# Attention with a mixture of experts on one core: 64 last rows in plain float32, w2 under a name per block, gathered rows turned in two runs

## The chip, the core and the metric

The kernel runs on one core of one Trainium2 chip. The metric is the device time of one execution in microseconds (us), lower is better. An engine is named as in the profile: PE is TensorE's matmuls and PEld its weight loads, DVE is VectorE, ACT is ScalarE, POOL is GpSimd, SP is SyncE, whose queue issues most transfers.

## What is computed

Causal attention with decay over 64 pairs of batch and head (576 positions, head size 64) gives 4608 rows of 512 numbers. Each row goes to one of eight experts, the one with the largest gate value.

```
logits = x @ w_gate                      # 4608 x 512 by 512 x 8
expert_idx = np.argmax(logits, axis=1)
for e in range(E):
    xe = x[expert_idx == e]
    h = np.maximum(xe @ w1[e], 0.0)      # 512 -> 1024
    ye = h @ w2[e]                       # 1024 -> 512
    out[mask] = gate_w[mask, None] * ye
```

## The kernel before

**Stages.** Attention fills the first 310 us; the change leaves it alone. Then eight places of experts follow, numbered e = 0 to 7. Places 2 to 7 hold experts sorted by how many rows they have. Each place has room for a fixed number of rows, `CAPS`: 640 for e = 0 to 3, then 608, 576, 576 and 512.

**Arithmetic.** To keep float32 accuracy with the faster type float32r, a number is split in a rounded part and a rest. A product is then three products: rounded by rounded, rounded by rest, rest by rounded.

**Up and down.** For e = 1 to 7, `seven` computes the hidden values: four rounds i of seven block products (Strassen's scheme) with 28 steps in all. After each of them other work may be inserted, by a table `ups` with the step's number. Then `down` multiplies hidden values with w2, one tile m of 128 rows after the other. A tile is four quarter tiles of six matmuls each (two of the eight row blocks of w2, times three products), 128 columns by 512. A second table, `dns`, says what is inserted after which quarter tile. The tables decide the order in which each engine gets its instructions; each engine works in that order.

**Rows of the next place.** While place e is in its stages, the rows of place e + 1 are gathered: `fetch(e + 1, m)` is an indirect transfer on POOL's queue that brings 128 rows (line 1172). Before, tiles 3 and 4 are fetched after step 6 of the up stage, tile 2 after step 13, tile 0 after step 20, and tile 1 after the first quarter tile of the down stage. `turn_t` transposes a tile on TensorE (four matmuls with the identity, line 1536) into one of two PSUM banks (`ps_t`), from which ACT and DVE build Strassen's sums (lines 1547 to 1561). POOL also adds up blocks of the next place's w1: `sums_s` (lines 1445 to 1448), four additions each, after steps 20 and 27 and after quarter tiles 7 and 14. `split_s` and `split_v` split blocks of w1 and w2: the cast on ACT (lines 1460, 1499), the rest on DVE (lines 1466, 1505).

**w2 in place.** `load_v` brings a block of w2 in float32 (512 KB, SP's queue, line 1485) into a region. `split_v` writes the rounded part to another region and the rest over the float32 values. Two neighbouring blocks share a name in each region; what waits for what is found by names.

**A buffer of the up stage.** In each round, a copy p5 of a product is made on ACT (line 1622), added to on POOL (line 1629) and read by DVE at last (line 1607, `hl<-u`). It has one buffer for all rounds.

Of the kernel before, what the change touches and what calls it, by code (L numbers as in the profile page):

```python
# [18 lines left out]
P = 128  # L19
# [23 lines left out]
NF = 2  # L43
SORTED = E - NF
CAPS = [CAP] * (E - 4) + [608, 576, 576, 512]
XN = ("T2", "T1", "T4", "T3", "B22")
# [65 lines left out]
def two_named(c, nc):  # L112
# [16 lines left out]
    for i, (nm, n) in enumerate(sizes):  # L129
# [3 lines left out]
        elif nm == "xT":  # L133
            name(("xT", i - 2), f"xT{i - 2}", n, at)
        elif nm == "aT":
            name(("aT", i - 5), f"aT{i - 5}", n, at)
            for k, (o, values) in enumerate(((0, False), (HW2, True))):
                name(("w2", i - 5, k), f"w2_{i - 5}_{k}", HW2, at + 4 * o, values)
            name(("hl", i - 5), f"hl{i - 5}", FT * (CA, CB)[i - 5], at, False)
            for k in range(2 * (i - 5)):  # L140
                name(("w1r", k), f"w1r{k}", 8 * P, at + 4 * (FT * CB + 8 * P * k))
        else:
            for k, (a, z) in enumerate(((0, 512), (512, 640))):
                name(("gT", k), f"gT{k}", z - a, at + 4 * a)
# [953 lines left out]
class Moe:  # L1098
# [127 lines left out]
    def sort_table(self):  # L1226
# [5 lines left out]
        for nm, x in (("gi", gi), ("si", si), ("g", g)):  # L1232
# [16 lines left out]
            mine.append(y)  # L1249
        self.idx["sorted"] = tuple(mine)  # L1250

# [84 lines left out]
    def down(self, e, m, part=(0, FT), pool=None):  # L1336
# [19 lines left out]
        self.scatter(y[0:n], si[0:n, s : s + 1])  # L1356


    def down_last(self, e, m):
# [118 lines left out]
    def w2_part(self, names, i, k):  # L1478

        return names["w2", i // 2, k][:, i % 2 * 2 * D : i % 2 * 2 * D + 2 * D]  # L1480

# [45 lines left out]

    def turn_t(self, e, m):

# [3 lines left out]
        xg = self.xg.pop((e, m))  # L1533
        pt = psum(c.ps_t)
        for kt in range(KT):
# [53 lines left out]
    def seven(self, e, i, run, tasks):  # L1589
# [6 lines left out]
        a, b, g, d = (t[:, 0:n] for t in (a, b, g, d))  # L1596
        p1, p5, u2, u3 = (self.up_.tile([P, HN], F32, name=f"u{k}")[:, 0:n] for k in range(4))
        hh, hl = self.h[e]

# [3 lines left out]
        def relu(src, *at):  # L1603
            A.activation(place(hh, *at), src, AF.Relu)

        def rest(src, *at):
            V.scalar_tensor_tensor(place(hl, *at), src, 0.0, place(hh, *at).bitcast(F32),
                                   ALU.max, ALU.subtract)

        def after(s):  # L1610
            if s == 0:
                if e == 1:
                    A.copy(p1, a)
                self.ends.pop(0)()
                if e > 1:
                    A.copy(p1, a)
                self.ends.pop(0)()
# [13 lines left out]
        def end():  # L1631
            relu(d, 1, 0)
            relu(p5, 1, 1)
            V.tensor_tensor(g, g, u2, ALU.add)
            rest(d, 1, 0)
# [8 lines left out]
        self.ends = [end, lambda: relu(g, 0, 1), lambda: (rest(p5, 1, 1), rest(g, 0, 1))]  # L1644

    def run(self, run, rest):
        c, tc = self.c, self.tc
        T = lambda f, *args: lambda: f(*args)
        fetch = lambda e, m: T(lambda: m * P < CAPS[e] and self.fetch(e, m))
        turn_t = lambda e, m: T(lambda: m * P < CAPS[e] and self.turn_t(e, m))  # L1650
        self.s, self.parts, self.slots = {}, {}, 0

        def downs(e, ms, tasks):
            k = 0
            for m in ms:
                for q in range(4):
                    run(lambda: self.down(e, m, (2 * q, 2 * q + 2)))
                    for f in tasks.get(k, []):
# [30 lines left out]
        with tc.tile_pool(name="moe_h", bufs=1) as hp, tc.tile_pool(name="moe_u", bufs=1) as up_, \  # L1689
                tc.tile_pool(name="moe_r", bufs=2) as self.wr:  # L1690
            self.up_ = up_
            hl = hp.tile([P, FT * CAP], F32R, name="hl")
            G = self.nc.gpsimd
            for e in range(1, E):
# [6 lines left out]
                def at(d, *items):  # L1701
# [6 lines left out]
                at(ups, (0, S(self.load_v, 0)), (0, S(self.load_v, 1)),  # L1708
                   (4, S(self.round_s, 2, 1)), (6, S(self.rest_s, 2, 1, G)),
                   (late, S(self.load_v, 2)), (late, S(self.load_v, 3)),  # L1710
                   (8, S(self.split_s, 3, 0)), (9, S(self.split_v, 0)),
                   (11, S(self.round_s, 3, 1)), (13, S(self.rest_s, 3, 1, G)),
                   (15, S(self.split_v, 1)), (v2, S(self.split_v, 2, last)),
                   *[(v3, S(self.split_v, 3))] * (e < E - 1))
                if e == 1:
                    at(ups, (0, S(self.sums_s, 3)), (2, S(self.split_s, 2, 0)))
                if e + 1 < E:
# [203 lines left out]
```

## Time and profile before

| | |
|---|---|
| median of three runs | 731.15 us (729.93 to 731.82) |
| profiled execution, its own time | 730.08 us |
| its span, first to last instruction | 728.1 us |
| PE busy | 718.9 us, 99% |
| DVE, ACT, POOL busy | 553.3, 480.2, 434.1 us |
| mean granted clock of TensorE | 0.999 of 2.4 GHz |

The span is what the trace covers; 2.0 us of the execution lie around it. PE's busy time counts a matmul from its start to its end, and neighbours overlap; what a matmul costs in a stream is the distance of starts.

### The profile page before, as it was taken

To read this page: it belongs to the slowest core of one execution; us is meant where nothing else is said; L and a number is where in the kernel's file an instruction comes from. 1 tells how busy PE (TensorE), PEld (TensorE's weight loads), DVE (VectorE), ACT (ScalarE), POOL (GpSimd) and SP (SyncE) were. 2 spreads that over 40 slices of the span, in tenths; PEclk is the share of its full clock that TensorE was granted. 3 is DMA by queue.
4 is the path that set the end of the run, shared out by engine and by line. 5 is a ranking of instruction groups with operands and counts; after the bars stand their busy time and mean duration, and the time that the engine had idled before them with its cause. 6 is when DMAs were issued, how large, how long until landed. Compare 5 with 4: busy or idle time off the path is not lost. (4 is left out here: it accounts for less than half of the span.)

```text
span 728.1 us, 16528 instructions
## 1 busy us (share of the span) xinstructions
PE 718.9 (99%) x5524; PEld 593.9 (82%) x5524; DVE 553.3 (76%) x1572; ACT 480.2 (66%) x1263; POOL 434.1 (60%) x593
## 2 busy tenths in 40 slices
PE   9999999999999999999999999999999999999996
PEld 6767777777777777889898898898898898898885
DVE  8877989898989899765989478488498498497460
ACT  7899998989898999433666366365365366365431
POOL 6644565656565576835777656566577476576421
PEclk9999999999999999999999999999999999999999
DMA  7988898888888886443383343443433433523301
GB/s 217 251 202 218 217 238 221 230 230 234 219 242 215 225 186 231 146 124 127 102 242 92 139 145 100 135 142 116 144 115 117 167 96 107 174 81 116 134 15 40
DMA packets 82694, 118.16 MB, mean 162 GB/s; under 512 B 9647, under 2 KB 40367, under 8 KB 82608
## 3 DMA queue, kind: packets, MB, share of 16 engines
q1 hardware_dynamic: 75680, 97.18, 48.1%
q0 software_dynamic: 6160, 19.67, 8.1%
q8 instruction: 45, 0.74, 0.4%
q14 instruction: 41, 0.34, 0.2%
q10 hardware_dynamic: 768, 0.25, 0.1%
HBM read 97.88 MB, written 19.63 MB: 161 GB/s over the span
## 5 line engine op out<-in xcount | busy, mean ns | idle before, releaser
L410 ACT ACTIVATE sc<-sc,nmx 128x128 f32<-128x128 f32 (+3 forms) x256 | 143.0, 567 | 2.1 <-DMA wraw<-in_w 1.0
L1583 PE MATMUL ps<-X_0w,w1s 128*128 128x320 f32 (+3 forms) x504 | 105.4, 300 | 0.7 <-ACT u L1622 0.7
L1348 PE MATMUL ps<-w_0w,hhw 128*128 128x512 f32 (+2 forms) x264 | 105.3, 399 | 0.0
L1348 PE MATMUL ps<-w_1w,hhw 128*128 128x512 f32 (+2 forms) x264 | 103.2, 391 | 0.3 <-DVE w_1w L1505 0.3
L1348 PE MATMUL ps<-w_0w,hl 128*128 128x512 f32 (+2 forms) x264 | 103.1, 391 | 0.0
L407 DVE CUSTOM_DVE_ANT_0 sc<-ps,dec 128x384 f32<-128x384 f32 (+2 forms) x192 | 90.2, 506 | 10.6 <-PE ps L423 2.8
L553 PE MATMUL ps<-aT,va_t 128*64 128x256 f32 (+3 forms) x896 | 92.1, 353 | 0.0
L553 PEld LDWEIGHTS ps<-aT,va_t 128*64 128x64 f32 x896 | 57.3, 137 | 31.9 <-issue 6.4
L1583 PEld LDWEIGHTS ps<-X_0w,w1s 128*128 128x128 f32 x504 | 81.7, 188 | 1.5 <-ACT u L1622 1.5
L423 PE MATMUL ps<-raw 64*128 64x256 f32 (+3 forms) x512 | 80.7, 444 | 0.4 <-ACT aT L489 0.4
L1583 PE MATMUL ps<-X_1w,w1s 128*128 128x320 f32 (+3 forms) x252 | 75.3, 299 | 0.0
L1380 POOL DMA_INDIRECT out<-y,so_si x29 | 30.4, 1049 | 72.4 <-ACT y L1355 51.2
L489 ACT COPY aT<-ps 128x512 f32<-128x512 f32 (+4 forms) x154 | 63.0, 453 | 12.5 <-PE ps L493 11.1
L423 PEld LDWEIGHTS ps<-raw 64*128 64x128 f32 x512 | 44.9, 186 | 25.8 <-issue 8.4
L1460 ACT CAST w1s<-w1r 128x1024 fp32r<-128x1024 f32 (+1 forms) x56 | 52.3, 948 | 11.1 <-POOL w1r L1446 10.8
L1466 DVE TENSOR_TENSOR w1s<-w1r,w1s 128x1024 fp32r<-128x1024 f32 (+1 forms) x42 | 52.2, 1257 | 9.2 <-ACT w1s L1460 9.2
L1355 ACT ACTIVATE y<-ps,so_gy 128x512 f32<-128x512 f32 (+2 forms) x28 | 19.3, 690 | 58.9 <-PE ps L1348 42.9
L1348 PEld LDWEIGHTS ps<-w_0w,hl 128*128 128x128 f32 (+2 forms) x264 | 48.5, 184 | 11.8
L1348 PEld LDWEIGHTS ps<-w_1w,hhw 128*128 128x128 f32 (+2 forms) x264 | 48.6, 184 | 10.9 <-DVE w_1w L1505 0.8
L487 DVE COPY aT<-ps 128x384 f32<-128x384 f32 (+4 forms) x118 | 54.2, 493 | 3.6 <-PE ps L493 1.7
L1348 PEld LDWEIGHTS ps<-w_0w,hhw 128*128 128x128 f32 (+2 forms) x264 | 48.5, 184 | 10.2
L1583 PE MATMUL ps<-xa,w1s 128*128 128x320 f32 (+3 forms) x336 | 55.2, 299 | 0.0
(309 smaller groups left out, 1772.9 us busy)
## 6 DMA issues: line engine op xcount, KB each, us to landing
dec<-cd SPq DMA_DIRECT2D x30, 512.0 KB, 5.8
w1r<-in_w SPq DMA_DIRECT2D x112, 128.0 KB, 3.3
w<-in_w SPq DMA_DIRECT2D x28, 512.0 KB, 4.6
raw<-in_qkT SPq DMA_DIRECT2D x63, 160.0 KB, 6.1
raw<-in_qkT SPq DMA_DIRECT2D x64, 144.0 KB, 4.9
decj<-cd SPq DMA_DIRECT2D x30, 288.0 KB, 5.0
va_t<-in_va SPq DMA_DIRECT2D x32, 256.0 KB, 5.7
x_dram<-row SPq DMA_DIRECT2D x32, 256.0 KB, 4.8
```

Source lines behind the costliest of these rows:

```text
L407: V.tensor_tensor_reduce(dst, src, m, -0.125, init, ALU.add, ALU.min, out)
L410: nc.scalar.activation(x, x, AF.Exp, bias=nmx, scale=-1.0, accum_out=acc)
L423: note(nc.tensor.matmul(banks[j][:, o : o + w], r[:, P * t : P * t + P], r[:, QW : QW + w], start=True, stop=n > 1))
L487: V.tensor_copy(dst, src)
L489: nc.scalar.copy(dst, src)
L553: c.last_av = note(nc.tensor.matmul(pv[j * HD : (j + 1) * HD, q0 - qa : qb - qa], l, r, start=(blk == 0), stop=(blk == nb - 1),))
L1348: c.note(nc.tensor.matmul(py, rows(hi_, ft), w[wi], start=(ft + k == 0), stop=(ft == FT - 1 and k == 2),))
L1355: nc.scalar.activation(y[0:n], py, AF.Copy, scale=g[0:n, s : s + 1])
L1380: self.nc.gpsimd.indirect_dma_start(out=self.out, out_offset=bass.IndirectOffsetOnAxis(ap=rows, axis=0), in_=y, in_offset=None, bounds_che ...
L1460: self.nc.scalar.copy(t[:, 0], raw)
L1466: (eng or self.nc.vector).tensor_tensor(lo, raw, hi.bitcast(F32), ALU.subtract)
L1583: self.nc.tensor.matmul(bank, w[:, wi, mat, kt], x[xi][:, kt, :], start=start and k == 0, stop=k == 5, skip_group_check=True,)
```

## The change

**Plain float32 for 64 rows.** Places 5 and 6 have 576 rows, so their fifth tile has 64. `down_few` now multiplies these with w2 in plain float32: no splitting, 16 matmuls of 64 columns by 256 in place of 24 of 64 by 512. The two halves of the 512 outputs go to PSUM partitions 0 to 63 and 64 to 127. The hidden values of these rows are kept unsplit (`keep`, 16 small activations on ACT for each of these places). The unsplit w2 is loaded again for blocks 0 to 2, into the region of the rests, as soon as tile 3 has read them; block 3 is added up from its parts (`whole_v`, DVE). For this, tiles 2 and 3 alternate quarter by quarter.

**Names.** Each block of w2 has its own name in each region.

**Turning.** The five tiles of the next place are turned in two runs: 3 and 4 after the first quarter tile, 2, 0 and 1 after the sixth, the last into a bank of another pool. Order and place of `fetch` stay.

**Smaller moves.** In the places without such a tile, p5 has a second buffer in rounds 1 and 3 (the space of `few`). For e = 1, `sums_s(1, 3)` moves from step 0 to 5, `split_s(1, 3, 0)` from 8 to 10, `split_v(1, 0)` from 9 to 8, and `copy(p1)` stands behind the ends of the round before.

```diff
+FEW = 64
-                name(("w2", i - 5, k), f"w2_{i - 5}_{k}", HW2, at + 4 * o, values)
+                for b in range(2):
+                    name(("w2", 2 * (i - 5) + b, k), f"w2_{2 * (i - 5) + b}_{k}", HW2 // 2,
+                         at + 4 * o + 2 * HW2 * b, values)
...
+    def down_few(self, e, m, q):
...
+        h, n = self.few(e), D // 2
+        if q == 0:
+            self.pf = psum(c.ps_s)
+        w = self.w2_part(c.values, q, 1).rearrange("p (f d) -> p f d", d=D)
+        for f in range(2):
+            for k in range(2):
+                nc.tensor.matmul(self.pf[k * FEW : k * FEW + FEW, 0:n], h[:, 2 * q + f],
+                                 w[:, f, k * n : k * n + n],
+                                 start=q + f == 0, stop=2 * q + f == FT - 1)
...
+        for k in range(2):
+            at = slice(k * FEW, k * FEW + FEW)
+            nc.scalar.activation(y[0:FEW, k * n : k * n + n], self.pf[at, 0:n], AF.Copy,
+                                 scale=g[at, s : s + 1])
+        self.scatter(y[0:FEW], si[0:FEW, s : s + 1])
...
+        if i % 2 and CAPS[e] % P != FEW:
+            p5 = self.few_rows.rearrange("p f s -> p (f s)")[:, 0:n]
...
+            if few:
+                todo[8:16] = [(m, q) for q in range(4) for m in (2, 3)]
...
-                    at(dns, (0, N(self.begin_t)), (0, turn_t(e + 1, 3)), (0, fetch(e + 1, 1)),
+                    at(dns, (0, N(self.begin_t)), (0, turn_t(e + 1, 3)), (0, turn_t(e + 1, 4)),
+                       (0, fetch(e + 1, 1)),
                        (0, N(self.split_s, 0, 0)), (1, N(self.split_s, 0, 1)),
-                       (2, N(self.load_s, 2)), (2, turn_t(e + 1, 4)),
-                       (3, N(self.split_s, 1, 0)), (4, turn_t(e + 1, 2)),
-                       (5, N(self.split_s, 1, 1)), (6, N(self.load_s, 3)),
-                       (6, turn_t(e + 1, 0)), (7, N(self.sums_s, 2)),
-                       (8, turn_t(e + 1, 1)), (9, N(self.split_s, 2, 0)),
+                       (2, N(self.load_s, 2)), 
+                       (4, N(self.split_s, 1, 0)),
+                       (5, turn_t(e + 1, 2)), (5, turn_t(e + 1, 0)),
+                       (5, turn_t(e + 1, 1, c.ps_s)), (5, N(self.split_s, 1, 1)), (6, N(self.load_s, 3)),
+                       (7, N(self.sums_s, 2)), (9, N(self.split_s, 2, 0)),
...
+                if self.few(e) is not None:
+                    at(dns, *((9 + 2 * i, S(self.load_v, i)) for i in range(3)),
+                       (15, S(self.whole_v, 3)))
```

On PE, in the down stage of place 4, the tiles of place 5 (`xg`) are turned between quarter tiles; before, tile 3's turn, then two quarter tiles, then tile 4's:

```order
L1348 MATMUL ps<-w_0_0w,hl 128x512
L1536 MATMUL ps<-identr,xg 128x128 x4
L1348 MATMUL ps<-w_0_0w,hhw 128x512
L1348 MATMUL ps<-w_0_1w,hhw 128x512
L1348 MATMUL ps<-w_0_0w,hl 128x512
```

In the changed kernel the same stage has eight such matmuls in that place, and twelve behind the sixth quarter tile (`w_1` is w2's second block, `w_2` its third), tile 1's at their end:

```order
L1355 MATMUL ps<-w_1_0w,hl 128x512
L1577 MATMUL ps<-identr,xg 128x128 x12
L1355 MATMUL ps<-w_2_0w,hhw 128x512
L1355 MATMUL ps<-w_2_1w,hhw 128x512
L1355 MATMUL ps<-w_2_0w,hl 128x512
```

Before, the last turn of the stage stood behind the ninth quarter tile; now it stands behind the sixth, three quarter tiles earlier.

On POOL, around the start of place 5's down stage, the changed kernel has this order: the fetch of tile 0, the last sum of the up stage, the four additions of `sums_s`, and only then the fetch of tile 1:

```order
L1175 DMA xg<-x_dram,so_gi 128x512
L1675 TENSOR_TENSOR u_8377<-u_8379,u_8377 128x288
L1486 TENSOR_TENSOR w1r<-w1r 128x256
L1487 TENSOR_TENSOR w1r<-w1r 128x256
L1488 TENSOR_TENSOR w1r<-w1r 128x256
L1489 TENSOR_TENSOR w1r<-w1r 128x256
L1175 DMA xg<-x_dram,so_gi 128x512
```

It is the order of before, with other line numbers: the fetch of tile 1 did not move, the turn that needs it did.

On PE, the end of place 5's down stage is now four groups of four plain float32 matmuls, each of another block of w2, where 24 rows of three products stood:

```order
L1355 MATMUL ps<-w_3_0w,hl 128x512
L1382 MATMUL ps<-w_0_1_95,few 64x256 x4
L1382 MATMUL ps<-w_1_1_97,few 64x256 x4
L1382 MATMUL ps<-w_2_1_104,few 64x256 x4
L1382 MATMUL ps<-w_3_1_106,few 64x256 x4
L1624 MATMUL ps<-xa,w1s 128x288 x6
```

Behind them the next place's up stage begins at once.

## Rows read from the trace of the kernel before

**Rows 1.** The page, part 1: engine, busy us, share, instructions.

```profile
PE 718.9 (99%) x5524; PEld 593.9 (82%) x5524; DVE 553.3 (76%) x1572; ACT 480.2 (66%) x1263; POOL 434.1 (60%) x593
```

**Rows 2.** Timeline of PE, place 5's down stage: start us, us, instruction.

```profile
599.15 0.46 PE L1536 MATMUL ps<-identr,xg 128*128 128x128 f32 x4
599.44 0.46 PE L1348 MATMUL ps<-w_0w,hhw 128*128 128x512 f32 x1
...
602.28 0.46 PE L1536 MATMUL ps<-identr,xg 128*128 128x128 f32 x4
...
611.94 0.47 PE L1348 MATMUL ps<-w_0w,hhw 128*128 128x512 f32 x1
...
621.55 0.40 PE L1348 MATMUL ps<-w_0w,hhw 128*64 128x512 f32 x1
...
627.08 0.95 PE L1583 MATMUL ps<-xa,w1s 128*128 128x288 f32 x6
```

**Rows 3.** Timeline of PE in attention: plain float32 products of 64 columns.

```profile
100.40 1.84 PE L553 MATMUL ps<-aT,va_t 128*64 128x256 f32 x16
102.07 0.29 PE L553 MATMUL ps<-aT,vb 68*64 68x64 f32 x4
```

**Rows 4.** Timeline of PE, first matmuls of the up stages of places 1, 2; ACT, DVE in place 1's.

```profile
360.57 1.04 PE L1583 MATMUL ps<-xa,w1s 128*128 128x320 f32 x6
...
415.47 1.04 PE L1583 MATMUL ps<-xa,w1s 128*128 128x320 f32 x6
...
371.94 0.42 ACT L1622 COPY u<-ps 128x320 f32<-128x320 f32 x1 [0.48 <-DVE hl L1607]
...
370.23 1.62 DVE L1607 SCALAR_TENSOR_TENSOR hl<-u,hhw 128x320 fp32r<-128x320 f32 x1 [0.69 <-ACT hhw L1604]
```

**Rows 5.** Timeline of POOL at the start of place 5's down stage.

```profile
599.92 1.78 POOL L1445 TENSOR_TENSOR w1r<-w1r 128x256 f32<-128x256 f32 x1
...
602.76 0.74 POOL L1447 TENSOR_TENSOR w1r<-w1r 128x256 f32<-128x256 f32 x1
603.47 1.80 POOL L1448 TENSOR_TENSOR w1r<-w1r 128x256 f32<-128x256 f32 x1
605.42 1.49 POOL L1172 DMA_INDIRECT xg<-x_dram,so_gi  x1
```

**Rows 6.** Fetches of places 2 to 7, then that of 605.42 alone: issue to landing.

```profile
DMA to landing us min/median/max: 3.3/4.0/5.9
...
DMA to landing us min/median/max: 4.6/4.6/4.6
```

**Rows 7.** Timeline of DVE, and of ACT, at the same place.

```profile
603.45 2.64 DVE L1466 TENSOR_TENSOR w1s<-w1r,w1s 128x1024 fp32r<-128x1024 f32 x2 [0.19 <-ACT w1s L1460]
...
604.03 0.28 ACT L1547 COPY X<-ps 128x128 f32<-128x128 f32 x1
```

**Rows 8.** Timeline of PE, tile 3's turn in places 1, 2, 4 and 6.

```profile
387.70 0.46 PE L1536 MATMUL ps<-identr,xg 128*128 128x128 f32 x4
...
441.49 0.46 PE L1536 MATMUL ps<-identr,xg 128*128 128x128 f32 x4
...
547.46 0.45 PE L1536 MATMUL ps<-identr,xg 128*128 128x128 f32 x4
...
650.58 0.45 PE L1536 MATMUL ps<-identr,xg 128*128 128x128 f32 x4
```

**Rows 9.** Timeline of POOL, the fetch of tile 1 in the same places.

```profile
392.48 1.77 POOL L1172 DMA_INDIRECT xg<-x_dram,so_gi  x1
...
445.37 1.76 POOL L1172 DMA_INDIRECT xg<-x_dram,so_gi  x1 [0.16 <-issue]
...
553.24 1.50 POOL L1172 DMA_INDIRECT xg<-x_dram,so_gi  x1
...
656.85 1.50 POOL L1172 DMA_INDIRECT xg<-x_dram,so_gi  x1 [0.16 <-issue]
```

**Rows 10.** Loads of w2's four blocks in place 5's up stage, issue to landing.

```profile
DMA to landing us min/median/max: 3.6/4.3/4.5
```

More of the change, by code (lines that the diff above doesn't have):

```diff
@@ L1249, in sort_table @@
             mine.append(y)
+        for s in range(n):
+            if CAPS[NF + s] % P == FEW:
+                k = s * NST + CAPS[NF + s] // P
+                V.tensor_copy(mine[2][FEW : 2 * FEW, k : k + 1], mine[2][0:FEW, k : k + 1])
         self.idx["sorted"] = tuple(mine)
@@ L1356, in down, with few, whole_v @@
         self.scatter(y[0:n], si[0:n, s : s + 1])
+    def few(self, e):
+        if CAPS[e] % P != FEW:
+            return None
+        return self.few_rows
+    def down_few(self, e, m, q):
+        c, nc = self.c, self.nc
+        _, si, g, s = self.index(e, m)
+        h, n = self.few(e), D // 2
[7 more added lines that the diff above has]
+                                 start=q + f == 0, stop=2 * q + f == FT - 1)
+        if q < 3:
+            return
+        y = c.yp.tile([P, D], F32, name="y")
+        for k in range(2):
[3 more added lines that the diff above has]
+        self.scatter(y[0:FEW], si[0:FEW, s : s + 1])
+    def whole_v(self, e, i):
+        c = self.c
+        hi, lo = (self.w2_part(c.words, i, k).bitcast(F32) for k in range(2))
+        self.nc.vector.tensor_tensor(self.w2_part(c.values, i, 1), hi, lo, ALU.add)
     def down_last(self, e, m):
@@ L1478, in w2_part @@
     def w2_part(self, names, i, k):
-        return names["w2", i // 2, k][:, i % 2 * 2 * D : i % 2 * 2 * D + 2 * D]
+        return names["w2", i, k]
     def load_v(self, e, i):
@@ L1526, in begin_t, with turn_t @@
         self.x[e] = t
-    def turn_t(self, e, m):
+    def turn_t(self, e, m, bank=None):
         c, nc = self.c, self.nc
@@ L1533, in turn_t @@
         xg = self.xg.pop((e, m))
-        pt = psum(c.ps_t)
+        pt = psum(bank or c.ps_t)
         for kt in range(KT):
@@ L1604, in relu, with keep @@
             A.activation(place(hh, *at), src, AF.Relu)
+        few = self.few(e)
+        def keep(src, f):
+            if few is not None:
+                A.activation(few[:, f * (FT // 2) + i], src[:, n - FEW : n], AF.Relu)
         def rest(src, *at):
@@ L1611, in after @@
             if s == 0:
-                if e == 1:
-                    A.copy(p1, a)
                 self.ends.pop(0)()
-                if e > 1:
-                    A.copy(p1, a)
+                A.copy(p1, a)
                 self.ends.pop(0)()
@@ L1633, in end @@
             relu(p5, 1, 1)
+            keep(p5, 1)
             V.tensor_tensor(g, g, u2, ALU.add)
@@ L1643, in seven @@
                 run(f)
-        self.ends = [end, lambda: relu(g, 0, 1), lambda: (rest(p5, 1, 1), rest(g, 0, 1))]
+        self.ends = [end, lambda: (relu(g, 0, 1), keep(g, 0)), lambda: (rest(p5, 1, 1), rest(g, 0, 1))]
     def run(self, run, rest):
@@ L1649, in run @@
         fetch = lambda e, m: T(lambda: m * P < CAPS[e] and self.fetch(e, m))
-        turn_t = lambda e, m: T(lambda: m * P < CAPS[e] and self.turn_t(e, m))
+        turn_t = lambda e, m, *bank: T(lambda: m * P < CAPS[e] and self.turn_t(e, m, *bank))
         self.s, self.parts, self.slots = {}, {}, 0
@@ L1654, in downs @@
             k = 0
-            for m in ms:
-                for q in range(4):
-                    run(lambda: self.down(e, m, (2 * q, 2 * q + 2)))
+            todo = [(m, q) for m in ms for q in range(4)]
+            few = e > 0 and self.few(e) is not None
+            if few:
+                todo[8:16] = [(m, q) for q in range(4) for m in (2, 3)]
+            for m, q in todo:
+                    if few and m == NST - 1:
+                        run(lambda: self.down_few(e, m, q))
+                    else:
+                        run(lambda: self.down(e, m, (2 * q, 2 * q + 2)))
                     for f in tasks.get(k, []):
@@ L1692, in run @@
             hl = hp.tile([P, FT * CAP], F32R, name="hl")
+            self.few_rows = hp.tile([P, FT, FEW], F32, name="few")
             G = self.nc.gpsimd
@@ L1708, in run @@
                 at(ups, (0, S(self.load_v, 0)), (0, S(self.load_v, 1)),
-                   (4, S(self.round_s, 2, 1)), (6, S(self.rest_s, 2, 1, G)),
+                   (4, S(self.round_s, 2, 1)),
+                       *[(5, S(self.sums_s, 3))] * (e == 1), (6, S(self.rest_s, 2, 1, G)),
                    (late, S(self.load_v, 2)), (late, S(self.load_v, 3)),
-                   (8, S(self.split_s, 3, 0)), (9, S(self.split_v, 0)),
+                   (10 if e == 1 else 8, S(self.split_s, 3, 0)),
+                       (8 if e == 1 else 9, S(self.split_v, 0)),
                    (11, S(self.round_s, 3, 1)), (13, S(self.rest_s, 3, 1, G)),
@@ L1715, in run @@
                 if e == 1:
-                    at(ups, (0, S(self.sums_s, 3)), (2, S(self.split_s, 2, 0)))
+                    at(ups, (2, S(self.split_s, 2, 0)))
                 if e + 1 < E:
```

## The prediction

> **What bounds the kernel now.** I read the page first: TensorE is busy 99% of the span [rows 1], so I look for matmuls that go away and for places where TensorE would have to wait. Then I read the timeline of one down stage, since nothing changes ahead of the first place's up stage. In place 5 the reader is to see how even the stream is: from 611.94 to 621.55 us stand 42 matmuls of 512 columns, 0.229 us each, and the 24 of the 64-row tile take from 621.55 to 627.08, 5.53 us, 0.230 each [rows 2]. So the 64 rows pay as much as 128. A turn costs more than its four matmuls: from 599.15 to 602.28 stand one turn and twelve matmuls, 3.13 us, of which the twelve are 12 x 0.229 = 2.75, so 0.38 is the turn's; the next matmul starts 0.29 after the turn's first [rows 2], so 0.09 is a restart. Last come the engines that TensorE would wait for: POOL, which issues the fetches, and DVE, which gets in its way.
>
> **The 64 rows.** The 24 matmuls go, twice (places 5 and 6). Instead 16 plain float32 products of 256 columns come, two halves side by side in partitions 0 to 63 and 64 to 127. Attention does this form already: line 553 multiplies two heads of 64 columns side by side, and the 16 records from 100.40 to 102.07 [rows 3] are eight such products (two records each), six of 256 and two of 192 columns, 1920 columns in 1.67 us, 0.87 ns each. Sixteen of 256 columns are 4096 columns, 3.56 us. Saved: 5.53 - 3.56 = 1.97 per place, **-3.9**. If the halves did not run side by side, it would be twice 3.56, 7.1 us, and the edit would cost 2 x 1.6 = 3.2. I take the first, since the form, the column count and the partitions are those of line 553.
>
> What these products wait for: blocks 0 to 2 of w2 are loaded again behind tile 3's use, in quarter tiles 9, 11 and 13. Block 2's is the tightest: after quarter tile 13 come two quarter tiles (2 x 6 x 0.229 = 2.75) and two groups of the new products (2 x 0.89), so it has 4.5 us; loads of that size took 3.6 to 4.5 from issue to landing [rows 10]. The wait is 0 to 0.5 per place with the issue; I take 0.1, **+0.2**. Block 3's sum on DVE starts when tile 3 has ended and costs about 1.3 (two rests of like size took 2.64, [rows 7]); three groups, 2.7 us, cover it. Were DVE late by more than that cover, TensorE would wait for the difference. The 16 small activations per place lie on ACT, which is busy two thirds of the span [rows 1]; where they still matter, see below. SP gets three loads more per place, ahead of the next place's loads of w2; those are used many steps later.
>
> **Two runs of turning.** There are 29 turns (five in places 1 to 5, four in place 6, whose successor has 512 rows) in 12 runs instead of 29, so 17 restarts of 0.09 go, 1.5 us. Inside a run the weight loads follow one another with little to hide under, which can take all of that back. Between 0 and -1.5 I take **-0.8**.
>
> **p5's second buffer.** The up stage of place 1 takes longer than that of place 2: from its first matmul to the first turn 387.70 - 360.57 = 27.13 us against 441.49 - 415.47 = 26.02 [rows 4, 8]. ACT's copy to p5 at 371.94 had waited for DVE's `hl<-u`, the last reader of the round before, 1.62 us long [rows 4]. With a second buffer that wait is gone in rounds 1 and 3, and round 2 finds its buffer free since long. **-1.1**; at worst nothing, if place 1's moved sums and splits make a wait of their own.
>
> **The turn that comes too early.** This is the step that decides. The turn of tile 1 needs the fetch of tile 1, which is on POOL's queue behind four additions, as before. Before, it stood behind the ninth quarter tile; now it stands in the second run, behind the sixth. Counted from the start of tile 3's turn: two turns of 0.31 (between 0.29 and 0.38), 30 matmuls of 0.229, two turns of 0.31: 8.1 us. In place 6, without a tile 4, 7.8.
>
> Against that stands when its rows land. In place 5 tile 3's turn starts at 599.15 [rows 2], the fetch at 605.42, that is 6.27 later [rows 5], and lands 4.6 after its start [rows 6]: 10.9. In places 1, 2, 4 and 6 the fetch starts 4.78, 3.88, 5.78 and 6.27 us after tile 3's turn [rows 8, 9]; with the same 4.6 it lands at 9.4, 8.5, 10.4 and 10.9. Late by: place 1 1.3, place 2 0.4, place 4 2.3, place 5 2.8, place 6 3.1. I take place 3 like place 2, 0.4. Sum 10.3 us, if POOL comes no earlier. TensorE stands still that long: matmuls are queued behind the turn, and no other engine gives the time back, since TensorE was the only one with no slack.
>
> Does POOL come earlier? The last addition before the fetch took 1.80 us, the one before it 0.74 [rows 5]. It began at 603.47, 0.02 behind the first of two rests on DVE that work from SBUF to SBUF [rows 7]. In the changed kernel ACT does tile 4's copies ahead of the casts that these rests wait for (before, the first of them stood behind, at 604.03, 0.28 long, [rows 7]), so the rests begin at least 0.28 later and the addition goes first. If it then takes 0.74, the fetch starts 1.06 earlier in places 4 and 5. In place 6 there is no tile 4, and only a small activation comes ahead; I take half, 0.5. In places 1 to 3 the fetch started earlier already. So 10.3 - 2 x 1.06 - 0.5 = **+7.7**. The Trainium skill, SBUF — State Buffer, section "SBUF: two separate sides", says the same of the cause: DVE and POOL share a pair of ports as an exclusive lock, and whichever starts first keeps it for its whole instruction. By that rule the sum is this 7.7, without it 10.3; the 1.80 beside 0.74 agrees.
>
> Bounds: if the fetches also land in 3.3, the fastest of all [rows 6], places 5 and 6 alone are late, by 0.4 and 0.7: +1.2 with rounding. If nothing comes earlier and place 1's POOL and DVE lag behind its shortened up stage by the 1.1 that it gains, 11.4.
>
> **Sum.** -3.9 + 0.2 - 0.8 - 1.1 + 7.7 = +2.1 us, on the profiled execution's own 730.08 (span 728.1 and 2.0 around it) 732.2. The median of the runs shown is 731.15, 1.07 above that execution, so 733.2 there. About 0.3%, 2.2 us (729.0 to 733.3), is what a measurement of this kernel can tell from no change.
>
> **The rivals.**
> - **The fetch comes in time (faster).** If POOL's queue runs ahead in the changed kernel, stalls shrink to 1 to 3 us and the sum is -4.5 to -2.5: 726.5 to 728.7. For it speaks that the additions are long only through DVE, whose order changes; against it that even the fastest landing leaves places 5 and 6 late. It decides from a fetch that starts 1.8 us earlier than now in place 5. Chance 0.22.
> - **Between the two.** Stalls of 3.5 to 5.5 us cancel the gain: 729 to 731. Chance 0.12.
> - **POOL comes no earlier, or later (slower).** Stalls of 9 to 12 us: 734.7 to 737.8. For it speaks place 6, and place 1, where DVE had no gap left near the end of the up stage; against it the order on ACT. Chance 0.17.
> - **The halves don't overlap (slower).** +3.2 in place of -3.9: 740.3. Line 553 speaks against it. Chance 0.04.
>
> **How the numbers follow.** The forecast itself (stalls of 5.5 to 9 us, 731 to 734.7, centre 733.2) has 0.45, of which about 0.30 lies within 0.3% and 0.15 above. Within 0.3%: 0.30 + 0.12 = 0.42. Slower: 0.15 + 0.17 + 0.04 = 0.36. Faster: 0.22. The sum of all lower bounds is -3.9 - 1.5 - 1.1 + 1.2 = -5.3, 725.8; of the upper ones, without the fourth rival, -3.9 + 1.0 + 11.4 = +8.5, 739.7. Eight times in ten I expect 727.3 to 737.3, which leaves out the ends of the first rival and the fourth.
>
> **What the profile after would show.** Right: two runs of transposes per down stage, a gap on TensorE ahead of the last four of the second run of about 1.3, 0.4, 0.4, 1.2, 1.8 and 2.6 us, put down to the fetch; place 5's last 16 products in about 3.6 us, two starting nearly together; place 1's up stage as long as place 2's; POOL's last addition at 0.74 in places 4 and 5. Wrong: second runs without a gap, products one after the other, or waits of the new products for w2's blocks or for DVE's sum of more than half a microsecond.

## The result, and the profile after

The changed kernel takes 741.49 us (median of four runs, 737.96 to 742.69), the kernel before, run beside it on the same chip, 731.49 (729.93 to 732.39). The ratio is 1.0133, with an interval of 1.0113 to 1.0152: ten microseconds slower, above the whole range of the prediction. The profiled execution took 742.20 us, with a span of 740.3.

The waits of TensorE come first (what PE waited for: us in total, times, longest):

```profile
PE ps L1624 <- ACT u L1662: 8.0, 3, 2.8
PE ps L1577 <- DMA xg<-x_dram,so_gi: 3.6, 3, 1.7
```

Line 1577 is the turn, line 1175 the fetch: the wait that the prediction was about. Line 1624 is the up stage's product, line 1662 ACT's copy p1, and this wait of 8.0 us the prediction did not have at all. Where the waits stand is seen in PE's timeline (start us, us, instruction, in brackets the idle time before it and what ended it):

```profile
361.32 1.04 PE L1624 MATMUL ps<-xa,w1s 128*128 128x320 f32 x6
...
379.73 1.15 PE L1624 MATMUL ps<-xa,w1s 128*128 128x320 f32 x6 [2.41 <-ACT u L1662]
...
390.04 0.79 PE L1577 MATMUL ps<-identr,xg 128*128 128x128 f32 x8
...
602.12 0.80 PE L1577 MATMUL ps<-identr,xg 128*128 128x128 f32 x8
...
609.67 0.79 PE L1577 MATMUL ps<-identr,xg 128*128 128x128 f32 x8
611.90 0.28 PE L1577 MATMUL ps<-identr,xg 128*128 128x128 f32 x1 [1.44 <-DMA xg<-x_dram,so_gi]
...
626.07 3.67 PE L1382 MATMUL ps<-w,few 128*64 128x256 f32 x32
629.68 1.06 PE L1624 MATMUL ps<-xa,w1s 128*128 128x288 f32 x6
...
641.47 1.81 PE L1624 MATMUL ps<-xa,w1s 128*128 128x288 f32 x6 [2.83 <-ACT u L1662]
...
657.66 0.46 PE L1577 MATMUL ps<-identr,xg 128*128 128x128 f32 x4
...
664.86 0.80 PE L1577 MATMUL ps<-identr,xg 128*128 128x128 f32 x8
667.35 0.53 PE L1577 MATMUL ps<-identr,xg 128*128 128x128 f32 x4 [1.69 <-DMA xg<-x_dram,so_gi]
...
683.08 3.67 PE L1382 MATMUL ps<-w,few 128*64 128x256 f32 x32
686.68 0.98 PE L1624 MATMUL ps<-xa,w1s 128*128 128x256 f32 x6
...
697.49 0.97 PE L1624 MATMUL ps<-xa,w1s 128*128 128x256 f32 x6 [2.76 <-ACT u L1662]
...
711.18 0.39 PE L1355 MATMUL ps<-w_0w,hhw 128*128 128x512 f32 x1
```

From an up stage's first product to tile 3's turn, place 6 takes 657.66 - 629.68 = 27.98 us where it took 650.58 - 627.08 = 23.50 [rows 2, 8], and place 1 takes 28.72 where it took 27.13 [rows 4, 8]. Place 7's up stage, up to the first product of its down stage, takes 24.50; in the trace of before it is 20.54.

To the waits comes a clock at half its rate. The windows view (PEclk, third column from the end, is the granted clock as a share of 2.4 GHz) has three such stretches ahead of the last stage:

```profile
629.68:640.90 11.22, 8.96 (x68) 8.72 (x66) 2.57 (x6) 3.77 (x9) 3.42 (x5) 1.00 0.65 218
640.90:644.30 3.40, 2.83 (x12) 2.83 (x13) 2.85 (x5) 3.40 (x10) 2.40 (x2) 0.50 0.20 57
...
668.20:671.60 3.40, 3.40 (x9) 2.65 (x9) 2.95 (x6) 1.03 (x2) 0.00 (x0) 0.50 0.41 124
...
698.90:702.30 3.40, 3.40 (x18) 3.38 (x17) 3.37 (x6) 1.98 (x4) 0.09 (x1) 0.50 0.03 5
```

The first begins within PE's wait of 2.83 us, the other two 0.9 and 1.4 us behind one. The price can be read in place 6's down stage: its 60 products behind the second run took 15.37 us, from the start of the first (667.71) to that of the float32 products behind them (683.08), the same 60 in place 5 13.81 (612.26 to 626.07), so 1.56.

The account of the two profiled executions, in us, from span to span (740.3 against 728.1): place 1 starts 0.75 later (361.32 where it was 360.57 [rows 4]), behind stages in which nothing changes, and the traces of the experiments have this start anywhere from 360.3 to 364.9; 64 rows -3.86 (3.60 per place where 5.53 stood [rows 2]); what the down stages of places 1 to 6 have more beside that and beside half clock, +4.08, all of it from tile 3's turn on, where the second runs wait; place 1's up stage +1.59; place 6's +4.48 and place 7's +3.96, half clock included; half clock in place 6's down stage +1.56; a wait of 0.33 for a block of w2 in place 7's down stage that is gone with the blocks' own names. The sum is +12.23, the difference +12.2.

**What happens at the end of places 5 and 6.** POOL's timeline shows it (line 1421 is the scatter of an output tile, 1486 to 1489 the additions of block 3, 1675 the sum for u of the next up stage):

```profile
625.79 1.00 POOL L1421 DMA_INDIRECT out<-y,so_si  x1 [5.11 <-ACT y L1362]
...
629.22 0.73 POOL L1489 TENSOR_TENSOR w1r<-w1r 128x256 f32<-128x256 f32 x1
630.10 1.01 POOL L1421 DMA_INDIRECT out<-y,so_si  x1 [0.15 <-issue]
638.75 0.93 POOL L1421 DMA_INDIRECT out<-y,so_si  x1 [7.64 <-PE pr L1624]
639.68 0.82 POOL L1675 TENSOR_TENSOR u<-u,u 128x288 f32<-128x288 f32 x1
```

Before, the last two scatters and the sum for u stood further apart, and the sum waited for DVE, not for a scatter:

```profile
622.92 1.00 POOL L1380 DMA_INDIRECT out<-y,so_si  x1 [0.15 <-issue]
628.28 0.93 POOL L1380 DMA_INDIRECT out<-y,so_si  x1 [4.36 <-ACT y L1355]
632.64 0.80 POOL L1629 TENSOR_TENSOR u<-u,u 128x288 f32<-128x288 f32 x1 [3.42 <-DVE u L1627]
```

Since tiles 2 and 3 alternate, the outputs of tiles 2, 3 and 4 are all ready within 5.3 us (ACT ends them at 625.51, 626.92 and 630.81). The scatter of 638.75 is that of the 64 rows. The page puts its wait of 7.64 us down to PE, but the transfer view has the scatter ahead of it, issued at 630.10, landing 7.9 us later, at 637.95:

```profile
DMA to landing us min/median/max: 7.9/7.9/7.9
```

The next scatter starts 0.80 us behind that landing, as it does in an experiment below with another landing (639.07, 639.87), and a row of another experiment names the scatter ahead as the releaser. All of them write the same tensor, at rows that are known only when the kernel runs. The sum for u stands behind it on POOL, and ACT's order hands the delay on to PE:

```profile
635.73 0.41 ACT L1647 ACTIVATE hhw<-ps 128x288 fp32r<-128x288 f32 x1 [0.52 <-DVE ps L1674]
640.54 0.44 ACT L1647 ACTIVATE hhw<-u 128x288 fp32r<-128x288 f32 x1 [4.40 <-POOL u L1675]
...
641.04 0.38 ACT L1662 COPY u<-ps 128x288 f32<-128x288 f32 x1
```

The copy p1 at 641.04, for which PE waits until 641.47, has nothing to do with this u; it only stands behind its activation.

### The profile page after: what moved, and what is told of

Same layout as the page of the kernel before. It is cut to its first block, busy times and chain, and to the rows that moved or that the text cites. A ratio compares the mean times of both kernels' runs of the same rounds, so it can differ in the third digit from the quotient of the medians.

```text
span 740.3 us, 16602 instructions
## 1 busy us (share of the span) xinstructions
PE 720.6 (97%) x5540; PEld 596.6 (81%) x5540; DVE 549.2 (74%) x1576; ACT 481.4 (65%) x1281; POOL 435.4 (59%) x593
## 5 line engine op out<-in xcount | busy, mean ns | idle before, releaser
L1355 PE MATMUL ps<-w_0w,hhw 128*128 128x512 f32 (+1 forms) x248 | 98.4, 397 | 0.0
L1355 PE MATMUL ps<-w_0w,hl 128*128 128x512 f32 (+1 forms) x248 | 97.6, 393 | 0.0
L1355 PE MATMUL ps<-w_1w,hhw 128*128 128x512 f32 (+1 forms) x248 | 97.4, 393 | 0.0
L1421 POOL DMA_INDIRECT out<-y,so_si x29 | 32.4, 1117 | 90.4 <-ACT y L1362 59.0
L1624 PE MATMUL ps<-xa,w1s 128*128 128x320 f32 (+3 forms) x336 | 57.0, 306 | 8.0 <-ACT u L1662 8.0
L1624 PEld LDWEIGHTS ps<-xa,w1s 128*128 128x128 f32 x336 | 50.2, 193 | 9.9 <-ACT u L1662 8.7
L1665 DVE TENSOR_TENSOR u<-ps,u 128x320 f32<-128x320 f32 (+3 forms) x28 | 13.1, 470 | 58.3 <-PE ps L1624 31.5
L1355 PEld LDWEIGHTS ps<-w_0w,hl 128*128 128x128 f32 (+1 forms) x248 | 46.6, 188 | 10.4
L1355 PEld LDWEIGHTS ps<-w_1w,hhw 128*128 128x128 f32 (+1 forms) x248 | 46.8, 189 | 10.0 <-DVE w_1w L1546 0.4
```

What stands on the lines that cost most here:

```text
L1355: c.note(nc.tensor.matmul(py, rows(hi_, ft), w[wi], start=(ft + k == 0), stop=(ft == FT - 1 and k == 2),))
L1421: self.nc.gpsimd.indirect_dma_start(out=self.out, out_offset=bass.IndirectOffsetOnAxis(ap=rows, axis=0), in_=y, in_offset=None, bounds_che ...
L1624: self.nc.tensor.matmul(bank, w[:, wi, mat, kt], x[xi][:, kt, :], start=start and k == 0, stop=k == 5, skip_group_check=True,)
L1665: V.tensor_tensor(u2, b, p1, ALU.add)
```

## The experiments

The theory: four losses, independent of one another, eat the gain of the 64 rows: the early turn, place 1's table, the pile of scatters at the end of places 5 and 6, and the clock behind the waits. The rivals: the up stages of places 6 and 7 are long for another reason (the early turns, ACT's additional activations, of which the trace has eight per place and not the sixteen that the prediction counts, the banks), or a loss that is taken away comes back elsewhere. All ratios below are against the kernel before, run on the same chip.

**Without the float32 path.** `few` returns nothing, all else stays.

```diff
-        if CAPS[e] % P != FEW:
-            return None
-        return self.few_rows
+        return None
```

> The changed kernel (742.2 us in its profiled execution) with the 64 rows multiplied as before, 24 products of three parts per place, tiles 2 and 3 one after the other, w2 not loaded twice; names, turning and place 1's order stay changed. Theory: the stretched up stages of places 6 and 7 (26.6 and 24.5 us, where 22.1 and 20.5 stood before) are the doing of the 64 rows' new path: their scatter stands on POOL's queue ahead of the sum for u and waits for tile 3's scatter. Then both stages fall back to 22.1 and 20.5 (-8.5 us), and the products cost 1.9 more per place (+3.8): 737.5. Rival, the early run of turns and the moved splits stretch these stages: they stay at 26.6 and 24.5 and the kernel takes 746.

Measured: 736.64 us, ratio 1.0073 (1.0037 to 1.0110). The up stages of places 6 and 7 are back at 22.12 and 20.24 us. So their stretch belongs to the 64 rows' path, and turning and names don't cause it. The kernel is still slower than before: its turns wait 5.1 us for their fetches, 3.4 of them in place 6.

**One scatter later.** The 64 rows' scatter is issued behind step 7 of the next up stage.

```diff
-        self.scatter(y[0:FEW], si[0:FEW, s : s + 1])
+        self.late = lambda: self.scatter(y[0:FEW], si[0:FEW, s : s + 1])
...
+                if e > 1 and self.few(e - 1) is not None:
+                    at(ups, (7, self.late))
```

> The changed kernel with one instruction moved: the scatter of the 64 rows is issued on POOL behind step 7 of the next place's up stage and no longer ahead of that stage's first sum for u. Theory: that sum then comes in time, the wait of PE for ACT's copy to u (about 3 us in each of places 6 and 7) and the two half-clock stretches behind it go: the up stages take 22.1 and 20.5 us, 742.2 - 8.5 = 733.7. Rival 1, ACT is what is late, for the 16 activations and the outputs of three tiles that now finish together: the copy is as late as before, 742. Rival 2, the scatter only carries its wait to step 7 and holds up the fetches and rests behind it: 736 to 740, with waits of PE in the second or third round of these stages.

Measured: 733.56 us, ratio 1.0016 (1.0002 to 1.0030), up stages of 22.22 and 20.37. The place of one instruction on POOL is worth 8 us. POOL's timeline of this kernel, at the same place:

```profile
632.64 1.00 POOL L1421 DMA_INDIRECT out<-y,so_si  x1 [0.15 <-issue]
637.89 0.80 POOL L1675 TENSOR_TENSOR u<-u,u 128x288 f32<-128x288 f32 x1 [4.25 <-ACT w1s L1501]
...
641.99 1.15 POOL L1421 DMA_INDIRECT out<-y,so_si  x1 [0.30 <-issue]
```

Tile 3's scatter is as slow as ever (it lands at 640.83, 8.19 us after its issue), but nothing that PE needs stands behind the wait: the sum for u starts 5.67 us after the stage's first product, 5.56 in the kernel before and 10.00 in the changed one. Both rivals fall: ACT had the same activations, and step 7 held nothing up.

**The copy ahead on ACT.** To see whether ACT's order is the link:

```diff
-                self.ends.pop(0)()
                 A.copy(p1, a)
                 self.ends.pop(0)()
+                self.ends.pop(0)()
```

> The changed kernel with the copy p1 ahead of the round before's last activations on ACT in all places; no scatter is moved. Theory: the link from POOL to PE is ACT's order, where p1 stands behind the activation of u that POOL still has to write. With p1 ahead, PE can go on to the last product of the round (two steps of 0.8 later in places 6 and 7, 0.9 in place 1), where the copy p5 behind the same activation holds it: the three waits of about 3 us shrink by 1.6 each, 737.4, and to 735 or less if the half-clock stretches go too. Rival, PE waits for a bank that the outputs y or the float32 products hold: unchanged, 742.

Measured: 741.23 us, ratio 1.0141 (1.0121 to 1.0160): no gain. But the wait has moved, as its row shows (line 1668 is the copy p5):

```profile
643.32 0.54 PE L1624 MATMUL ps<-X_0w,w1s 128*128 128x288 f32 x2 [2.79 <-ACT u L1668]
```

PE did get two steps further. The copy p5 then stood behind the late activation and behind another activation and a cast of 1.04 us, which ACT had put off too, so it came as much later as PE had gained. That the chain runs over ACT's order is confirmed; that the waits shrink by 1.6 each was wrong (only place 1's did shrink, from 2.41 to 1.48 us).

**Why tile 3's scatter is slow.** First try: w2's loads for places 6 and 7 stand behind later steps.

```diff
-                at(ups, (0, S(self.load_v, 0)), (0, S(self.load_v, 1)),
+                l = (4, 5, 8, 9) if e > 1 and self.few(e - 1) is not None else (0, 0, late, late)
+                at(ups, (l[0], S(self.load_v, 0)), (l[1], S(self.load_v, 1)),
...
-                   (late, S(self.load_v, 2)), (late, S(self.load_v, 3)),
+                   (l[2], S(self.load_v, 2)), (l[3], S(self.load_v, 3)),
```

> The changed kernel with w2's four loads of places 6 and 7 behind steps 4, 5, 8 and 9 of their up stage and no longer behind steps 0, 0, 1 and 1; the scatters stay where they are. Theory: tile 3's scatter takes 7.85 us to land since these 2 MB share the DMA engines with it; without them it lands in some 4, the 64 rows' scatter is issued that much earlier, and of the 3 us that PE waits in each of the two stages 0 to 0.5 are left: 734 to 735, if the splits of w2 are not late in turn. Rival, the scatter is slow by itself, or the loads of w1 are enough to slow it: places 6 and 7 keep 26.6 and 24.5, 742.

Measured: 740.95 us, ratio 1.0142 (1.0109 to 1.0174). This tells nothing of the cause, since the edit did not do what it was to do: SP's queue issued the four loads at the same time as ever, 2.5 us ahead of the up stage's first product, as soon as the float32 products had read their region.

```profile
628.01 2.96 SPq L1526 DMA_DIRECT2D w<-in_w  x4
```

Second try: ACT issues them, behind steps 3 to 6, in its own order.

```diff
-        self.nc.sync.dma_start(
+        (eng or self.nc.sync).dma_start(
...
+                l, q = (0, 0, late, late), None
+                if e > 1 and self.few(e - 1) is not None:
+                    l, q = (3, 4, 5, 6), self.nc.scalar
+                at(ups, (l[0], S(self.load_v, 0, q)), (l[1], S(self.load_v, 1, q)),
```

> The changed kernel with w2's four loads of places 6 and 7 issued by ACT behind steps 3 to 6 of their up stage. In the earlier try with other steps SP issued them at the same time as ever, since SP runs ahead of the steps and waits only for the region that it fills; ACT issues in its own order, so here they do start some 2 to 5 us after the first step. The scatters stay where they are. Theory: tile 3's scatter has the DMA engines for itself and lands some 3 to 4 us after its issue, not 7.9; the 64 rows' scatter is issued some 4 us earlier, and PE's waits of 2.8 and 3.0 us in places 6 and 7 go with their half-clock stretches: up stages of 22 to 23 and 20.5 to 21.5, 734 to 735.5. Rival, the scatter is slow without the loads too: it lands in 7 to 8 us, the two stages stay at 26.6 and 24.5, 741 to 742. Should w2's first block now be late for its split, PE would wait in the second round instead.

Measured: 732.66 us, ratio 1.0022 (1.0006 to 1.0039), up stages of 22.22 and 20.34. The scatters stand where they stood in the changed kernel:

```profile
629.85 1.00 POOL L1421 DMA_INDIRECT out<-y,so_si  x1 [0.15 <-issue]
633.35 0.93 POOL L1421 DMA_INDIRECT out<-y,so_si  x1 [2.50 <-DMA out<-y,so_si]
635.10 0.80 POOL L1675 TENSOR_TENSOR u<-u,u 128x288 f32<-128x288 f32 x1 [0.81 <-DVE u L1673]
```

The second scatter now waits 2.50 us, and this time the row names the scatter ahead of it. So the loads of w2 are what made tile 3's scatter slow, and taking away either the crowding or the place on POOL frees both stages. The edit changed the loads' time and their queue at once: ACT issues the first at 632.31, when the last of tile 3's packets has gone (632.21), so that the later time is enough is shown, and what another queue does by itself is not.

**Tile 1's turn back behind the ninth quarter tile.**

```diff
-                       (5, turn_t(e + 1, 1, c.ps_s)), (5, N(self.split_s, 1, 1)), (6, N(self.load_s, 3)),
-                       (7, N(self.sums_s, 2)), (9, N(self.split_s, 2, 0)),
+                       (5, N(self.split_s, 1, 1)), (6, N(self.load_s, 3)),
+                       (7, N(self.sums_s, 2)), (8, turn_t(e + 1, 1, c.ps_s)), (9, N(self.split_s, 2, 0)),
```

> The changed kernel with the turn of tile 1 behind the ninth quarter tile, where it stood before; tiles 2 and 0 stay behind the sixth. Theory: the waits for the fetch (together about 4.5 us) go, and with place 6's wait of 1.9 also the stretch of 3.41 us at half the clock from 668.2 us on, worth 1.6: 736.1. Rival 1, that stretch has another cause: 737.7. Rival 2, POOL is as late as before and the wait only moves to what follows the turn (the sums of Strassen's scheme that the next up stage needs): 742.

Measured: 737.54 us, ratio 1.0084 (1.0056 to 1.0112). Among PE's waits from place 1's down stage to place 6's (395 to 690 us) there is no fetch any more, only the wait in place 6's up stage:

```profile
PE ps L1624 <- ACT u L1662: 3.0, 1, 3.0
```

And place 6's down stage runs at the full clock (windows view), so the first rival falls:

```profile
671.00:686.00 15.00, 15.00 (x85) 11.70 (x85) 8.23 (x13) 5.79 (x9) 7.26 (x10) 1.00 0.67 199
```

Its down stages of places 5 and 6 take 27.33 and 27.04 us, where 29.32 and 28.89 stood before the change: with the wait gone, the 64 rows' 1.9 is all there. The three tiles could not be turned earlier than the fetch allows, and turning them together gains nothing: places 2 and 3 took 29.15 and 29.07 us, 29.09 and 29.09 before. The median alone would not tell the expectation (736.1) from the first rival (737.7), since its interval reaches from 735.5 to 739.6; in the profiled execution, 741.61, place 1 starts 3.56 us later than in the changed kernel's trace, and half clock follows place 1's wait, so its own time doesn't tell either; its clock in place 6 does.

**Place 1's table as before**, with p5's second buffer kept.

```diff
+                if e == 1:
+                    A.copy(p1, a)
                 self.ends.pop(0)()
-                A.copy(p1, a)
+                if e > 1:
+                    A.copy(p1, a)
...
-                       *[(5, S(self.sums_s, 3))] * (e == 1), (6, S(self.rest_s, 2, 1, G)),
+                   (6, S(self.rest_s, 2, 1, G)),
...
-                   (10 if e == 1 else 8, S(self.split_s, 3, 0)),
-                       (8 if e == 1 else 9, S(self.split_v, 0)),
+                   (8, S(self.split_s, 3, 0)),
+                       (9, S(self.split_v, 0)),
...
-                    at(ups, (2, S(self.split_s, 2, 0)))
+                    at(ups, (0, S(self.sums_s, 3)), (2, S(self.split_s, 2, 0)))
```

> The changed kernel with place 1's table as before (sums of block 3 behind step 0, its split at 8, w2's at 9, the copy p1 ahead of the ends); p5's second buffer stays. Theory: the moved work makes the one wait of 2.7 us at 379.7, and the second buffer alone takes away the two waits of 0.5 that place 1 had: its up stage falls from 27.3 to 24.7 us, 739.6. Rival 1, the second buffer alone gains nothing (25.7 as before): 740.6. Rival 2, the wait comes from the second buffer (POOL writes it while DVE holds their common ports): the stage stays at 27.3, 742.2.

Measured: 740.82 us, ratio 1.0106 (1.0077 to 1.0136). PE's first product and first turn of place 1 in this kernel:

```profile
360.87 1.04 PE L1624 MATMUL ps<-xa,w1s 128*128 128x320 f32 x6
...
387.33 0.80 PE L1577 MATMUL ps<-identr,xg 128*128 128x128 f32 x8
```

26.46 us from the one to the other, 2.26 less than the changed kernel and 0.67 less than before [rows 4, 8]: the buffer gains 0.7, not the 1.0 expected here, and the moved table loses more than that. 1.5 us of the gain go to the turn of tile 1, which in place 1 now waits for its fetch.

**Only the four additions back** behind step 0, the other moves of place 1 kept.

```diff
-                       *[(5, S(self.sums_s, 3))] * (e == 1), (6, S(self.rest_s, 2, 1, G)),
+                   (6, S(self.rest_s, 2, 1, G)),
...
-                    at(ups, (2, S(self.split_s, 2, 0)))
+                    at(ups, (0, S(self.sums_s, 3)), (2, S(self.split_s, 2, 0)))
```

> The changed kernel with one of place 1's moves undone: the four additions of its block 3 stand behind step 0 again, the splits and the copy p1 stay moved. Theory: the additions, behind step 5, push POOL's sum for u in the following rounds back, and ACT's copy p1, now behind the activation of that u, passes it on to PE; without them place 1's up stage takes 25.1, as with the whole table undone, 740. Rival, the copy p1 behind the ends is enough: the stage stays above 26.5, 742.

Measured: 739.92 us, ratio 1.0116 (1.0077 to 1.0155). Place 1's up stage takes 25.53 us, between the two: of the 2.26, the additions on POOL explain 1.8; for the last 0.47 the moved copy and splits are left, not told apart. With the moved table the stage takes 27.3 in the changed kernel and 28.8 with the later scatter. The wait in it is 2.41 us in both, but with the later scatter half clock follows it (windows view):

```profile
381.00:384.40 3.40, 3.40 (x14) 3.40 (x14) 3.13 (x6) 1.79 (x4) 1.74 (x2) 0.50 1.08 323
```

Without the float32 path the stage takes 26.1, with a wait of 1.24. Why that wait is shorter is open.

**All three repairs together** (later scatter, tile 1's turn, place 1's table).

> The three edits together (tile 1's turn behind the ninth quarter tile, the scatter of the 64 rows behind step 7 of the next place, place 1's table as before). Theory: the three losses are independent, and what is left of the change is its gain: place 5's and 6's down stages 2.0 and 1.85 us shorter than before, place 7's 0.3, place 1's up stage 0.7, turning in runs nothing: 731.4 - 4.9 = 726.5. Rival: one loss hides another (with the waits gone DVE, ACT or POOL cannot keep pace and TensorE waits elsewhere): 728.5 to 731.

**The 64 rows and the names alone**, with the later scatter; turning, place 1's table and p5 as in the kernel before. Against the kernel above:

```diff
-        if i % 2 and CAPS[e] % P != FEW:
-            p5 = self.few_rows.rearrange("p f s -> p (f s)")[:, 0:n]
...
-                    at(dns, (0, N(self.begin_t)), (0, turn_t(e + 1, 3)), (0, turn_t(e + 1, 4)),
-                       (0, fetch(e + 1, 1)),
+                    at(dns, (0, N(self.begin_t)), (0, turn_t(e + 1, 3)), (0, fetch(e + 1, 1)),
...
+                       (2, N(self.load_s, 2)), (2, turn_t(e + 1, 4)),
+                       (3, N(self.split_s, 1, 0)), (4, turn_t(e + 1, 2)),
...
+                       (6, turn_t(e + 1, 0)), (7, N(self.sums_s, 2)),
+                       (8, turn_t(e + 1, 1)), (9, N(self.split_s, 2, 0)),
```

> Of the change only the 64 rows in float32 and the names stay, with their scatter behind step 7 of the next place; turning table, place 1's table and p5's one buffer as before. Theory: 731.4 - 4.1 = 727.3, and the three edits together are 0.7 faster than this, by p5's second buffer in place 1 alone. Rival, turning in runs is worth the 0.8 and the buffer the 1.1 of the prediction: this kernel is 1.9 slower than the three edits together.

Measured: all three repairs 726.72 us, ratio 0.9944 (0.9927 to 0.9960); the 64 rows and the names alone 726.51, ratio 0.9940 (0.9925 to 0.9955). Both beat both kernels, by 4.2 to 4.4 us against before and by 15 against the change as it was made. In the first, PE has 99% of the span again:

```profile
PE 714.6 (99%) x5540; PEld 591.8 (82%) x5540; DVE 550.4 (76%) x1576; ACT 481.4 (67%) x1281; POOL 431.8 (60%) x593
```

Taken singly, the three repairs lower the ratio by 0.0117, 0.0049 and 0.0027, 0.0193 in sum, and together by 0.0189: the losses are independent. What pays is the float32 path, with the names, which no run takes apart from it (the 0.33 in place 7 is theirs). The 0.7 between the two that p5's buffer should make shows in the traces (place 1's up stage 25.07 against 25.75), but not in the medians. The down stages are alike (places 1 to 4: 29.11, 29.07, 29.15, 29.59 in runs, 29.16, 29.09, 29.09, 29.57 one by one), so turning in runs is worth nothing.

## Why the prediction was wrong

- **The 64 rows.** Right, mechanism and size: 3.60 us per place, predicted 3.56, and no wait for a block of w2 or for DVE's sum, where 0.1 had been allowed. The rival that the halves don't overlap falls.
- **The step that failed** is in the same part, where the prediction lists what the edit drags along: it counted the new products' own waits, the activations on ACT and the loads on SP ("those are used many steps later"), and stopped there. The third queue that the edit touches, POOL's, was left out, its scatters put at nothing without a reason. Alternating tiles 2 and 3 brings three scatters close together, SP's loads of 2 MB make the second one last 7.9 us, the third waits for it, and the next up stage's sum stands behind. The loads are not late for their reader; they are in the way of somebody else's transfer. This cost 8.4 us in places 6 and 7, most of the 10.0 by which the profiled execution (742.2) is above its sum (732.2). The two experiments that free the chain at either end come to 733.56 and 732.66; that this is the forecast's 733.2 owes something to the other errors, which nearly cancel.
- **The turn that comes too early.** Right in mechanism, too large in size: 7.7 predicted, 4.5 measured. The second runs lose 0.19, 0.03, 0.05, 0.70, 1.65 and 1.90 in places 1 to 6 (predicted 1.3, 0.4, 0.4, 1.2, 1.8, 2.6). POOL does come earlier, by about the 1.06 that had been taken: in place 5 the fetch starts 5.24 us after tile 3's turn, where it was 6.27 [rows 2, 5], and the addition ahead of it is down from 1.80 to 0.74. It starts 0.44 us ahead of DVE's rest (606.91), where it stood 0.02 behind one, as the rule cited there had it (the Trainium skill, SBUF — State Buffer, section "SBUF: two separate sides").

```profile
606.47 0.74 POOL L1489 TENSOR_TENSOR w1r<-w1r 128x256 f32<-128x256 f32 x1
607.36 1.77 POOL L1175 DMA_INDIRECT xg<-x_dram,so_gi  x1
```

 In place 6 the gain was the same 1.1 (5.16 against 6.27 [rows 8, 9]), not the half that had been taken. In places 1 to 3 fetches that were sooner done than the 4.6 us taken for all left almost no wait: in places 2 and 3 they landed 4.34 and 4.45 us after their start; in place 1 the fetch came 4.83 us after tile 3's turn, no sooner than before (4.78 [rows 8, 9]), but POOL was busy with it for 0.96 us where it had been 1.77.
- **Runs of turning, -0.8.** 0.4 at most, by which the 4.08 of the account is under the 4.5 that the second runs lose, and nothing in the kernel with all three repairs: the value should have been the upper bound, nothing.
- **p5's second buffer, -1.1.** 0.7 by itself, once place 1's table is put back. The clause "at worst nothing, if place 1's moved sums and splits make a wait of their own" was too mild. They did make one, and it cost 1.6 more than before: a bound that stops at zero was no bound.
- **The clock.** Not in the prediction at all: the waits were priced by their length. Behind some of them the clock halves, which in place 6's down stage added 1.56 us to a wait of 1.69, and in the up stages of places 6 and 7 most of what their 8.4 have beyond the waits of 2.83 and 2.76.

By the spans the change cost 12.2 where the sum has 2.1. Of the 10.1 between them, the chain over POOL makes 8.4. The mis-sized terms (turn -3.2, table and buffer +2.7, runs +0.4, clock in the down stage +1.6, the 64 rows' waits -0.2, the names -0.3) and the 0.75 of place 1's later start come to +1.7 together.

## What to carry to other kernels

When an edit changes the order in which results become ready, follow each result to its store: here the stores of one tensor went one after another, and the engine that issued one held everything behind it until the store ahead had landed. Count not only whether a load that is moved comes in time for its reader, but which transfer it fills the DMA engines against. A queue that runs ahead of the other engines (SP's here) wasn't delayed by writing its instructions later; to delay a transfer, issue it from an engine that gets there later.

## What the runs showed of the hardware that was not expected

**A scatter of POOL's got no turn while SP's loads ran.** It was issued from 630.10 to 631.11. The transfer view of 631 to 634.8 us in the changed kernel has one queue alone, SP's; the scatter's packets start at 634.85, 78 of its 80 are through at 636.25 and the last two at 637.26. The scatter before it, with hardly a load beside it, had its first packet 1.57 us after its start (627.36 for 625.79); this one waited 4.75, 3.2 longer. SP's is q1 (queue, kind: packets, MB, share of 16 engines):

```profile
DMA packets 589, 1.14 MB, mean 300 GB/s; under 512 B 32, under 2 KB 32, under 8 KB 589
...
q1 hardware_dynamic: 589, 1.14, 90.1%
```

With the loads on ACT, whose first packet comes at 633.39, the scatter's 80 packets (q0) are through within 631 to 634:

```profile
q0 software_dynamic: 80, 0.26, 21.4%
```

The Trainium skill, DMA: Bandwidth & Descriptors, section "Queues, rings and completion order", says that each DMA engine takes turns between the queues that have work, packet by packet. By that the scatter's packets would have run between those of the loads; here none did for 3.2 us. It isn't always so: without the float32 path tile 3's scatter, issued at 625.32 as the same loads set in, shares 628 to 629 us with them:

```profile
q0 software_dynamic: 79, 0.26, 63.5%
q1 hardware_dynamic: 71, 0.12, 38.7%
```

Whether the packets of the slow scatter were held back in the DMA engines, or their descriptors came late, the trace doesn't tell. In the kernel before, a scatter took up to 6.49 us at the same place (the one of 628.28), but nothing waited for it.

**The same wait can leave the clock alone.** Place 1's wait of 2.41 us left the clock alone in the changed kernel and was followed by half clock with the later scatter. With place 6's turn it is the other way round: with the later scatter it waited 1.8 us, as long as in the changed kernel (1.69). The waits of that kernel's PE from 595 us on:

```profile
PE ps L1577 <- DMA xg<-x_dram,so_gi: 3.2, 2, 1.8
```

But the clock stayed at 1.00 (windows view):

```profile
664.00:684.00 20.00, 18.42 (x101) 14.37 (x102) 10.08 (x18) 7.65 (x13) 9.08 (x12) 1.00 0.65 199
```

What decides between the two was not settled.
